# A masked-attention and feed-forward kernel: the causal mask of one half batch, the chunk marks and part of the ELU moved to GpSimd, with new instruction lists

## The chip, the cores and the metric

The kernel runs on one core of a Trainium2 chip. The metric is the device time of one launch in microseconds. The engines are TensorE (PE in the profile, its weight loads PEld), VectorE (DVE), ScalarE (ACT), GpSimd (POOL) and SyncE (SP), which here only issues DMAs.

## The reference

Four batches of eight heads, 768 positions, 64 elements per head. Attention sees, for each query, only the six chunks of 32 keys with the greatest upper bound, under the causal mask; the result goes through a feed-forward layer with an ELU.

```python
k_min, k_max = min, max of k over each chunk of 32      # 24 chunks
ub = sum_d max(q * k_min, q * k_max)                     # [B,H,S,24], later chunks -1e9
top_chunks = argsort(ub)[..., -6:]
scores = q @ k.T / 8
mask = (chunk of key in top_chunks) & (query pos >= key pos)
attn = softmax(where(mask, scores, -1e9))
x = (attn @ v) as [3072, 512]
h = x @ w_in                                             # 512 -> 2048
g = where(h > 0, h, exp(min(h, 0)) - 1)
out = g @ w_out                                          # 2048 -> 512
```

## The kernel before

Heads go in pairs: unit u is a pair of heads, 16 units, four per batch. A unit's queries and each batch's feed-forward layer are cut into two halves of 384 rows.

Per unit there is a preparation. For batch 0 (`first_prep`, per half) keys and queries are loaded in rows and turned by TensorE (L696); ScalarE copies the turned keys (L706) and queries (L728, and L732 with a Relu), VectorE takes minimum and maximum of each chunk (L715), and GpSimd casts queries (L748) and values (L739). For batches 1 to 3 (`pair_prep`) the loads arrive in blocks and VectorE turns them (L615, L633), with the same work behind (L619, L649, L748).

The choice of chunks (`quad_sel`) works for two units at a time: the bounds by TensorE (L782), then VectorE transposes (L798), finds the eight largest (L810), compares (L815) and transposes back (L821), and GpSimd puts the flags of the chunks that are not chosen (L832) into rows 64 to 87 of the query operand. The key operand carries in the same rows the chunk marks, -40000 in row c for keys of chunk c. The score matmul (L874) has these 88 rows, so that a key of a chunk not chosen gets a large negative score. The marks are made once as `econ` (L531) and copied by VectorE into the five buffers of the key operand (L542).

`pair_attend` makes the transposed scores of one half: TensorE writes a piece into PSUM (two buffers S2), ScalarE takes the exponential (L901), TensorE multiplies by the values (L933), VectorE normalises (L946, L949). The diagonal blocks need a triangular mask. In batch 0 (`onpe`) TensorE adds a triangle of -40000 by a second matmul with the identity (L880) into the same bank; in the other batches GpSimd zeroes the triangle behind the exponential by an affine select (L920). The result is turned, by TensorE (L982) and a ScalarE copy (L985), or for some halves through DRAM.

`mlp` makes for each half 16 blocks of 128 features: `up` matmuls (L1011) into one of three PSUM banks H, exponential by ScalarE (L1020), then the ELU in one of three ways. The usual one for batches 0 to 2 takes two VectorE operations that both read PSUM, t = max(e - 1, h) at L1049 and gT = min(max(h, 0), t) at L1054. For the blocks named in `BOTH`, ScalarE makes a Relu in place (L1025) and VectorE one operation (L1028). In batch 3 (`FAST`) two blocks are taken at once in S2: VectorE makes t = min(e, 1) - 1 (L1038), and gT = max(t, h) (L1043). The bank comes free with the last of these. `down` matmuls (L1070) sum 16 blocks into M (MT in batch 3), ScalarE copies (L1079), SP stores.

The order of all this is not left to a scheduler: `QUEUE` lists, for each engine, the numbers of its operations in the order in which it runs them, and each engine works its list strictly from the front. `Plan.order` only places the buffers of the pools by it. The lists of SP (loads and stores) and of GpSimd also hold the DMA issues, among GpSimd's those of the weights (L570, L574), 0.5 MB each.

Of the kernel before, what the change touches and what calls it, by code (L numbers as in the profile page):

```python
# [11 lines left out]
AOT = mybir.AluOpType  # L12
# [5 lines left out]
H = 8  # L18
# [20 lines left out]

BOTH = {0: (1, 5, 9, 13), 1: (0, 1, 2, 3, 4, 5, 8, 9, 10, 11, 12, 13), 2: (1, 5, 9, 13), 3: ()}  # L40
# [7 lines left out]
TRIPE = True  # L48
KCAST = ['ACT', 'ACT']

# [23 lines left out]
    ],  # L74
    "POOL": [
# [10 lines left out]
    ],  # L86
    "ACT": [
# [19 lines left out]
    ],  # L107
# [7 lines left out]
    ],  # L115
# [284 lines left out]
def kernel(  # L400
# [129 lines left out]
    def c_econ():  # L530
        nc.scalar.activation(out=econ[64:96].rearrange("p (c w) -> p c w", w=CHUNK),  # L531
                             in_=ident_f[64:96, 64:64 + NCH].unsqueeze(2).to_broadcast([32, NCH, CHUNK]),
                             func=AF.Copy, scale=MASKNEG)
# [619 lines left out]
```

## Time and profile before

| what | value |
|---|---|
| median of 3 runs | 268.43 us (268.42 to 268.64) |
| profiled execution, first to last instruction | 266.7 us |
| left between the two, outside the span | 1.7 us |
| TensorE busy | 256.0 us, 96% |
| VectorE busy | 211.6 us, 79% |
| ScalarE busy | 195.8 us, 73% |
| GpSimd busy | 118.0 us, 44% |
| HBM over the span | 135 GB/s |

The profile records one execution; no own time is given for it beside its span, so that the span is set against the median of the runs. A group's line shows its source line, engine, operation, output and inputs, shape and count, then its busy time, the mean of one in ns, and the engine's idle time ahead of it with what ended it. A line of the timeline shows the start, the time and the same names. Matmuls are pipelined: one is recorded as busy for longer than the next one has to wait behind it.

### The profile page before, as it was taken

How to read it: one execution, taken by the hardware profiler on the slowest of the kernel's cores; microseconds unless marked ns; L12 is line 12 of the kernel's file. 1: busy time of each engine (PE TensorE's matmuls, PEld its weight loads, DVE VectorE, ACT ScalarE, POOL GpSimd, SP SyncE). 2: the span in 40 equal slices, each digit the busy share in tenths (PEclk: the TensorE clock that was granted, in tenths of full speed). 3: DMA queues.
4: the chain of work that ended last, by engine and by line, in shares of the span. 5: the costliest groups of instructions: out<-in, count | busy, mean ns of one | idle time of the engine just before them, and what ended most of it. 6: DMA issues, size and time to landing. Idle time of an engine off the chain costs nothing.

```text
span 266.7 us, 6618 instructions
## 1 busy us (share of the span) xinstructions
PE 256.0 (96%) x2393; PEld 159.4 (60%) x2420; DVE 211.6 (79%) x544; ACT 195.8 (73%) x363; POOL 118.0 (44%) x208
## 2 busy tenths in 40 slices
PE   4999999999999999999999999999999999999994
PEld 3887766755565556655565555655666555565543
DVE  4897999999999999899997858986779676227640
ACT  4899899955987789997899549787988842433421
POOL 2588774163896898952934157524250000000000
PEclk9999999999999999999999999999999999999999
DMA  6999999999998999999403561040102300210123
GB/s 206 272 238 155 205 194 202 196 147 177 198 153 134 163 204 159 152 167 186 106 7 77 175 172 18 15 125 15 58 11 59 116 2 0 79 42 0 39 81 118
DMA packets 121264, 32.15 MB, mean 121 GB/s; under 512 B 108304, under 2 KB 118288, under 8 KB 121232
## 3 DMA queue, kind: packets, MB, share of 16 engines
q1 hardware_dynamic: 115920, 26.75, 51.3%
q0 software_dynamic: 4224, 4.19, 10.0%
q10 hardware_dynamic: 1088, 0.79, 0.9%
q8 instruction: 19, 0.31, 0.5%
q14 instruction: 13, 0.11, 0.2%
HBM read 28.44 MB, written 7.47 MB: 135 GB/s over the span
## 4 chain that ended last, share of the span: by engine, by line
PE 83%; DVE 5%; ACT 5%; DMA 4%; issue 2%; SPq 0%; DVEq 0%; ACTq 0%
PE psH L1011 20%; PE psM L1070 20%; PE psS L874 11%; PE psS L1011 8%; PE psMT L1070 8%; PE psO L933 7%; PE psS L782 3%; DMA f<-in_v_dram 3%; PE psH L696 2%; PE psMT L696 2%; ACT pt L901 2%; DMA gT<-in_k_dram 1%; ACT lhs L706 1%; PE psT L982 1%; DVE thr L810 1%
## 5 line engine op out<-in xcount | busy, mean ns | idle before, releaser
L901 ACT ACTIVATE pt<-psS 128x768 bf16<-128x768 f32 (+1 forms) x120 | 89.1, 778 | 11.9 <-PE psS L874 7.3
L1011 PE MATMUL psH<-xT,w_in_sb 128*128 128x384 bf16 x384 | 75.0, 326 | 0.3
L1070 PE MATMUL psM<-w_out_sb,gT 128*128 128x512 bf16 x264 | 67.9, 379 | 1.3
L1011 PEld LDWEIGHTS <-w_in_sb 128*128 128x128 bf16 x512 | 47.6, 97 | 34.4 <-issue 1.4
L1070 PEld LDWEIGHTS <-gT 128*128 128x128 bf16 x400 | 37.8, 98 | 34.4 <-DVE gT L1054 0.5
L1020 ACT ACTIVATE f<-psH 128x384 f32<-128x384 f32 x96 | 47.8, 509 | 12.5 <-PE psH L1011 10.1
L920 POOL TENSOR_SCALAR_AFFINE_SELECT pt<-pt 128x512 bf16<-128x512 bf16 (+1 forms) x48 | 24.8, 529 | 69.0 <-ACT pt L901 61.9
L874 PE MATMUL psS<-rhs,lhs 88*128 88x384 bf16 (+4 forms) x304 | 54.2, 283 | 0.8 <-ACT pt L901 0.6
L874 PEld LDWEIGHTS <-lhs 88*128 88x128 bf16 x304 | 27.9, 97 | 15.4 <-ACT pt L901 1.9
L1049 DVE SCALAR_TENSOR_TENSOR t<-f,psH 128x384 bf16<-128x384 f32 x56 | 30.5, 546 | 6.3 <-ACT f L1020 5.8
L748 POOL CAST rhs<-f 64x768 bf16<-64x768 f32 (+1 forms) x40 | 27.9, 702 | 14.1 <-DVE f L633 6.6
L933 PEld LDWEIGHTS <-pt 128*128 128x128 bf16 x672 | 27.5, 98 | 7.5 <-issue 0.9
L1054 DVE SCALAR_TENSOR_TENSOR gT<-psH,t 128x384 bf16<-128x384 f32 x56 | 30.6, 551 | 1.2
L933 PE MATMUL psO<-vext,pt 128*128 128x65 bf16 x672 | 29.6, 194 | 0.2 <-DVE gT L1054 0.2
L748 POOL CAST lhs<-f 64x768 bf16<-64x768 f32 x24 | 19.7, 822 | 18.6 <-PE psS L874 12.3
L832 POOL COPY rhs<-selt 24x576 bf16<-24x576 bf16 (+2 forms) x40 | 22.7, 567 | 8.6 <-DVE selt L821 5.8
L1020 ACT ACTIVATE f<-psS 128x768 f32<-128x768 f32 x16 | 13.0, 811 | 18.0 <-PE psS L1011 17.9
L1028 DVE SCALAR_TENSOR_TENSOR gT<-f,psH 128x384 bf16<-128x384 f32 x40 | 21.4, 542 | 5.3 <-ACT psH L1025 5.3
L1011 PE MATMUL psS<-xT,w_in_sb 128*128 128x384 bf16 x128 | 22.6, 326 | 0.0
L1070 PE MATMUL psMT<-w_out_sb,gT 128*128 128x512 bf16 (+1 forms) x109 | 22.1, 348 | 0.2
L1025 ACT ACTIVATE psH<-psH 128x384 f32<-128x384 f32 x40 | 20.7, 520 | 0.0
L949 DVE TENSOR_TENSOR on<-psO,rc 128x384 bf16<-128x384 f32 x32 | 17.6, 554 | 0.8
(56 smaller groups left out, 270.9 us busy)
## 6 DMA issues: line engine op xcount, KB each, us to landing
out_dram<-osb SPq DMA_DIRECT2D x23, 256.0 KB, 2.5
f<-in_k_dram SPq DMA_DIRECT2D x48, 96.0 KB, 3.9
f<-in_q_dram SPq DMA_DIRECT2D x48, 96.0 KB, 3.8
f<-in_v_dram SPq DMA_DIRECT2D x24, 192.0 KB, 4.0
w_in_sb<-in_moe_w_in_dram POOLq DMA_DIRECT2D x4, 512.0 KB, 7.9
w_out_sb<-in_moe_w_out_dram POOLq DMA_DIRECT2D x4, 512.0 KB, 8.4
gT<-in_k_dram SPq DMA_DIRECT2D x8, 192.0 KB, 4.4
gT<-in_v_dram SPq DMA_DIRECT2D x12, 128.0 KB, 3.9
```

The lines of the kernel that those rows point to most:

```text
L748: nc.gpsimd.tensor_copy(out=o, in_=i)
L832: eng.tensor_copy(out=dst.rearrange("c h (i two x) -> c h i two x", two=2, x=32)[:, :, :, odd, :], in_=tiles[st][r0:r0 + NCH, c0:c0 + n].r ...
L874: nc.tensor.matmul(p_s[:, hd, pc:pc + w], lhsT=tiles[pt_["kb"]][0:64 + NCH, hd, 128 * kb:128 * kb + 128], rhs=tiles[pt_["qb"]][0:64 + NCH, ...
L901: lambda bs=bs, pt=pt, wtot=wtot, lo=lo, at=at: nc.scalar.activation(out=tiles[pt][:, :, lo:lo + wtot], in_=tiles[bs[0]][:, :, at:at + wto ...
L920: nc.gpsimd.affine_select(out=a, in_=a, compare_op=AOT.is_ge, fill=0.0, base=0, pattern=pat, channel_multiplier=-1)
L933: nc.tensor.matmul(po[:, hd, qi, :], lhsT=tiles[pt][:, hd, off:off + 128], rhs=tiles[pt_["vx"]][:, 6 * hd + kb, :], start=(kb == 0), stop= ...
L1011: nc.tensor.matmul(o, lhsT=w_in_sb[:, kk, f0:f0 + 128], rhs=rhs, start=(kk == 0), stop=(kk == NKK - 1))
L1020: lambda e=e, view=view: nc.scalar.activation(out=halves(e)[:, 0:step], in_=view(), func=AF.Exp),
L1028: lambda e=e, view=view, fc=fc, gt=gt: nc.vector.scalar_tensor_tensor(out=tiles[gt][:, fc:fc + step, :], in0=halves(e)[:, 0:step], scalar= ...
L1049: lambda e=e, t=t, view=view: nc.vector.scalar_tensor_tensor(out=tiles[t][:, 0:step], in0=halves(e)[:, 0:step], scalar=1.0, in1=view(), op ...
L1054: lambda t=t, view=view, fc=fc, gt=gt: nc.vector.scalar_tensor_tensor(out=tiles[gt][:, fc:fc + step, :], in0=view(), scalar=0.0, in1=tiles ...
L1070: nc.tensor.matmul(pm, lhsT=tiles[gt][:, fc, 128 * tt:128 * tt + 128], rhs=w_out_sb[:, fc, x0:x1], start=(fc == 0), stop=(fc == NFC - 1))
```

## The change

Four things change. The triangular mask by TensorE stays for the first half of batch 0 alone (`TRIPE`); its second half takes GpSimd's affine select, as the other batches do. The chunk marks are made by GpSimd instead of ScalarE. For 24 blocks of the feed-forward layers of batches 0 to 2 (`POOLED`, four in each half, all of them blocks with two VectorE operations before) GpSimd makes t = min(e, 1) - 1 and VectorE gT = max(t, h). And the lists of all five engines are new; the numbers in them shift, because eight affine selects are added in the plan. The further lines of the diff are a variant of the key copies that is switched off (`KTWO`), tags, and a constant that moves.

```diff
+POOLED = {(0,0):(2,6,10,14),(0,1):(2,6,10,14),(1,0):(6,7,14,15),(1,1):(6,7,14,15),(2,0):(2,6,10,14),(2,1):(2,6,10,14)}
-TRIPE = True
+TRIPE = (0,)
+KTWO = False
 QUEUE = {
...
     def c_econ():
-        nc.scalar.activation(out=econ[64:96].rearrange("p (c w) -> p c w", w=CHUNK),
-                             in_=ident_f[64:96, 64:64 + NCH].unsqueeze(2).to_broadcast([32, NCH, CHUNK]),
-                             func=AF.Copy, scale=MASKNEG)
+        nc.gpsimd.tensor_scalar(out=econ[64:96].rearrange("p (c w) -> p c w", w=CHUNK),
+                                in0=ident_f[64:96, 64:64 + NCH].unsqueeze(2).to_broadcast([32, NCH, CHUNK]),
+                                scalar1=MASKNEG, scalar2=None, op0=AOT.mult)
...
-                onpe = u in SPLIT and TRIPE
+                onpe = u in SPLIT and hf in TRIPE
...
+                if fc in POOLED.get((b, hf), ()):
+                    add("POOL", pool(step * HALF), pr,
+                        lambda e=e, t=t: nc.gpsimd.tensor_scalar(
+                            out=tiles[t][:, 0:step], in0=halves(e)[:, 0:step], scalar1=1.0, scalar2=1.0,
+                            op0=AOT.min, op1=AOT.subtract),
+                        reads=[(e, 0)], writes=[t], alloc=[t], free=[e])
+                    add("DVE", dve(step * HALF), pr,
+                        lambda t=t, view=view, fc=fc, gt=gt: nc.vector.tensor_tensor(
+                            out=tiles[gt][:, fc:fc + step, :], in0=tiles[t][:, 0:step], in1=view(), op=AOT.max),
+                        reads=[t, bh[0]], writes=[(gt, fc + i) for i in range(step)],
+                        alloc=[gt] if fc == 0 else [], free=bh + [t])
+                    continue
```

The new lists, by their beginnings (before, after):

```diff
     "DVE": [
-        0, 6, 11, 9, 12, 8, 10, 22, 23, 38, 7, 39, ...
+        0, 10, 9, 11, 6, 7, 22, 23, 8, 12, 38, 24, ...
     "POOL": [
-        1, 5, 4, 3, 28, 29, 44, 45, 46, 62, 30, 63, 179, 78, 80, 79, 87, 64, 178, 86, 89, 195, 129, 194, 128, 127, 88, 130, 213, 331, ...
+        3, 1, 4, 2, 44, 45, 5, 62, 28, 30, 29, 46, 339, 78, 63, 79, 178, 341, 89, ...
     "SP": [
-        13, 31, 163, 47, 65, 165, 17, 215, 181, 51, 217, 183, 197, 199, 201, 167, 517, ...
+        13, 31, 47, 65, 163, 183, 17, 165, 197, 215, 181, 199, 217, 51, 544, 167, 542, ...
```

Here 2 is `econ`, 6 VectorE's fills of the query operand, 7 the identity's cast, 8 to 12 the copies of the marks, 22 and 23 the first chunk bounds; 331 (before) and 339 (after) the first weight transfer; 17, 51, 167 and 201 loads of values, 517 and 544 the first loads of batch 1, the others of SP loads of keys and queries of batch 0. On TensorE the first `up` of batch 0 stands behind five score pieces of unit 0's second half, one of unit 1's and one value tile before, and behind the five of unit 0 alone after.

More of the change, by code (lines that the diff above doesn't have):

```diff
@@ L47 @@
 PUTS = False
-TRIPE = True
+TURN = ((2, 0), (2, 1), (3, 0),)
+TRIPE = (0,)
 KCAST = ['ACT', 'ACT']
+KTWO = False
 EARLY = (4, 0)
@@ L545 @@
     add("POOL", 0.4, -9.5, c_ident, reads=["fill"], writes=["ident"])
-    add("ACT", 0.7, -9.0, c_econ, reads=["ident"], writes=["econ"])
+    add("POOL", 0.95, -9.0, c_econ, reads=["ident"], writes=["econ"])
     add("POOL", 1.0, -8.9, c_kept, writes=["kept"])
@@ L586, in fetch @@
         add("DMA", 0.0, pr, lambda: None, reads=[w], writes=writes, lat=plan.LANDED)
-    TURN = ((2, 0), (2, 1), (3, 0),)
     PAIR = {}
@@ L687, in first_prep, with kview, turn @@
             fetch(3, 512, 256, pl + 1.55, vload, [(sv, iv), (sv, iv + 1)], alloc=[sv] if u == SPLIT[0] and hf == 0 else [])
-        bk, bq = bank("H"), bank("MT")
-        def turn(bb, i):
+        bk, bq = new("S2") if KTWO else bank("H"), bank("MT")
+        def kview():
+            return tiles[bk[0]][:, 0, 0:HALF] if KTWO else ps(bk, [P, HALF], F32)
+        def turn(view, i, twice=False):
             def f():
-                p_ = ps(bb, [P, HALF], F32)
+                p_ = view()
                 for n in range(3):
@@ L697, in f @@
                                             tiles[sg][:, i, o:o + 64 + 64 * hd], ident_f)
-            return f
-        add("PE", 0.65, pr, turn(bk, i0), reads=[(sg, i0), "ident"], writes=[bk[0]], alloc=bk)
-        for hd in range(2):
+                    if twice:
+                        nc.tensor.transpose(tiles[bk[0]][0:64, 1, 0:HALF].rearrange("p (t j) -> p j t", j=3)[:, n],
+                                            tiles[sg][:, i, 192 + 64 * n:256 + 64 * n], ident_f)
+            return f
+        add("PE", 0.97 if KTWO else 0.65, pr, turn(kview, i0, KTWO), reads=[(sg, i0), "ident"], writes=[bk[0]], alloc=bk)
+        if KTWO:
+            add("ACT", act(S), pr,
+                lambda: nc.scalar.activation(out=tiles[kb][0:64, :, a:b], in_=tiles[bk[0]][0:64, :, 0:HALF], func=AF.Copy),
+                reads=[bk[0]], writes=[(kb, hf, 0), (kb, hf, 1), (bk[0], "turn")], alloc=[] if hf else [kb], tag="ktwo")
+        for hd in () if KTWO else range(2):
             by = KCAST[hf] if hd else "ACT"
@@ L707, in first_prep @@
                         out=o(), in_=ps(bk, None, None)[64 * hd:64 * hd + 64, :], func=AF.Copy),
-                    reads=[bk[0]], writes=w, alloc=al)
+                    reads=[bk[0]], writes=w, alloc=al, tag="kcopy%d" % hd)
             else:
@@ L716, in first_prep @@
                     out=tiles[kx][:, 0:12] if x else tiles[km][:, 0, c],
-                    in_=ps(bk, None, None).rearrange("p (c w) -> p c w", w=CHUNK),
+                    in_=kview().rearrange("p (c w) -> p c w", w=CHUNK),
                     axis=mybir.AxisListType.X, op=op),
@@ L724, in first_prep @@
             reads=[kx, (km, 0, hf)], writes=[(km, 1, hf)], free=[kx], port=True)
-        add("PE", 0.65, pr + 0.05, turn(bq, i0 + 1), reads=[(sg, i0 + 1), "ident"], writes=[bq[0]], alloc=bq,
+        add("PE", 0.65, pr + 0.05, turn(lambda: ps(bq, [P, HALF], F32), i0 + 1), reads=[(sg, i0 + 1), "ident"], writes=[bq[0]], alloc=bq,
             free=[sg] if u == SPLIT[-1] else [])
@@ L728, in first_prep @@
             lambda: nc.scalar.activation(out=tiles[qt][:, a:b], in_=ps(bq, None, None), func=AF.Copy),
-            reads=[bq[0]], writes=[qt], alloc=[qt])
+            reads=[bq[0]], writes=[qt], alloc=[qt], tag="qcopy")
         lo = max(a, SEL0)
@@ L733, in first_prep @@
                                          func=AF.Relu),
-            reads=[bq[0]], writes=[qa], alloc=[qa], free=bq)
+            reads=[bq[0]], writes=[qa], alloc=[qa], free=bq, tag="qrelu")
         for hd in range(2):
```

176 rows, old and new, of the table QUEUE are left out of this document.

## The prediction

> **What bounds the kernel now.** I read the page first, then busy time by stretches, then the order of TensorE's instructions, then the groups by shape. The page's busy shares:
>
> ```profile
> span 266.7 us, 6618 instructions
> PE 256.0 (96%) x2393; PEld 159.4 (60%) x2420; DVE 211.6 (79%) x544; ACT 195.8 (73%) x363; POOL 118.0 (44%) x208
> ```
>
> TensorE is busy 96% of the span; GpSimd has more than half of its time free. The stretches show how that is spread:
>
> ```profile
> 0.00:31.40 31.40, 26.20 (x380) 22.34 (x381) 24.33 (x106) 25.88 (x57) 21.11 (x55) 1.00 1.05 216
> 31.40:60.00 28.60, 28.24 (x308) 18.16 (x309) 26.78 (x62) 24.52 (x47) 14.20 (x23) 1.00 1.25 186
> 60.00:110.00 50.00, 49.39 (x462) 29.41 (x467) 49.44 (x129) 41.96 (x79) 38.68 (x60) 1.00 1.01 166
> ```
>
> The columns are the stretch, its length, then busy time of PE, PEld, DVE, ACT and POOL, the granted clock (1.00 in all), and the DMA. Up to 31.4 us, where the first matmul of the feed-forward part stands, TensorE lacks 5.2 us, 4.0 of them ahead of its first instruction; in the two stretches behind it lacks 0.4 and 0.6. From 60 to 110 VectorE is as full (49.44 of 50) as TensorE (49.39), and GpSimd is at 38.68.
>
> A busy TensorE is not yet one at its peak, because an instruction's end is modelled. What one matmul costs when others queue behind it is the step from start to start:
>
> ```profile
> 30.41 0.22 PE L874 MATMUL psS<-rhs,lhs 88*128 88x128 bf16 x1
> 30.47 0.22 PE L880 MATMUL psS<-trineg,ident_b 128*128 128x128 bf16 x1
> 30.53 0.22 PE L874 MATMUL psS<-rhs,lhs 88*128 88x128 bf16 x1
> 30.59 0.22 PE L880 MATMUL psS<-trineg,ident_b 128*128 128x128 bf16 x1
> 59.75 2.54 PE L1070 MATMUL psM<-w_out_sb,gT 128*128 128x512 bf16 x11
> 62.13 0.81 PE L1011 MATMUL psH<-xT,w_in_sb 128*128 128x384 bf16 x4
> 29.70 0.45 PE L933 MATMUL psO<-vext,pt 128*128 128x65 bf16 x9
> ```
>
> A mask matmul (L880) of 128 columns takes 0.22 us by itself but 0.058 us of the queue (30.41 to 30.59 in three steps: 0.06). In the same way L1070 costs (2.54 - 0.38) / 10 = 0.216, L1011 (0.81 - 0.33) / 3 = 0.161, L933 (0.45 - 0.19) / 8 = 0.032. With these steps I ask how full TensorE really is from 60 to 110:
>
> ```profile
> L1011 PE MATMUL psH<-xT,w_in_sb 128*128 128x384 bf16 x92 | 18.3, 326 | 0.0
> L1070 PE MATMUL psM<-w_out_sb,gT 128*128 128x512 bf16 x69 | 17.8, 379 | 0.4
> L874 PE MATMUL psS<-rhs,lhs 88*128 88x384 bf16 (+2 forms) x78 | 13.7, 288 | 0.1
> L933 PE MATMUL psO<-vext,pt 128*128 128x65 bf16 x138 | 6.0, 194 | 0.2 <-DVE gT L1054 0.2
> L982 PE MATMUL psT<-ident_b,on 128*128 128x128 bf16 x21 | 2.2, 219 | 0.0
> L782 PE MATMUL psS<-f,km 64*32 64x288 f32 x32 | 1.4, 415 | 0.0
> ```
>
> 92 x 0.161 + 69 x 0.216 + 138 x 0.032 + 21 x 0.058 (as the mask's 128 columns) = 35.3. The 78 score matmuls come in widths 384, 256 and 128 as 10 : 4 : 4 and cost by their columns 0.125 on average, 9.8 together. The bound computations (L782) take 1.4 for this operand, and with the other one, which overlaps it, I count 2.3. That is 47.4; for some five L1070 that the trace lacks (a few per cent of the matmul records are missing) I add 1.1. So about 1.5 us of these 50 are waits hidden in busy time; TensorE sets the pace, and VectorE, full as well, is the next that could.
>
> **The change part by part.** First, the mask matmuls of batch 0's second half. Each of its four pairs has three diagonal blocks for two heads, six mask matmuls, 24 in all. Where they lie (columns: PE busy and count, PEld the same):
>
> ```profile
> 26.00:31.40 5.40, 1.06 (x6) 0.58 (x6) 1.00 1.36 201
> 31.40:40.00 8.60, 1.06 (x6) 0.66 (x7) 1.00 1.35 198
> 40.00:50.00 10.00, 1.65 (x9) 0.90 (x10) 1.00 1.36 204
> 50.00:60.00 10.00, 0.47 (x4) 0.20 (x3) 1.00 1.06 158
> ```
>
> Six lie before 31.4, where TensorE has idle time anyway; I take nothing for them (at most 6 x 0.058 = 0.35). The other 18 lie where it has none: 18 x 0.058 = 1.04 us off the path. In their place each pair gets two affine selects on GpSimd, one of 256 and one of 512 elements, between the exponential on ScalarE and the value matmuls. Their price, and that of everything else that moves, stands in the groups by shape:
>
> ```profile
> L920 POOL TENSOR_SCALAR_AFFINE_SELECT pt<-pt 128x512 bf16<-128x512 bf16 x24 | 15.5, 650 | 51.6 <-ACT pt L901 51.0
> L920 POOL TENSOR_SCALAR_AFFINE_SELECT pt<-pt 128x256 bf16<-128x256 bf16 x24 | 9.6, 407 | 17.5 <-ACT pt L901 10.9 <-PE psH L1011 5.2 <-PE psO L933 1.1
> L739 POOL CAST vext<-gT 128x384 bf16<-128x384 f32 x8 | 4.1, 509 | 1.0 <-DMA gT<-in_v_dram 0.9
> L748 POOL CAST lhs<-f 64x768 bf16<-64x768 f32 x24 | 19.7, 822 | 18.6 <-PE psS L874 12.3 <-DVE rc L946 4.6 <-DVE f L615 0.9
> L1049 DVE SCALAR_TENSOR_TENSOR t<-f,psH 128x384 bf16<-128x384 f32 x56 | 30.5, 546 | 6.3 <-ACT f L1020 5.8
> L1054 DVE SCALAR_TENSOR_TENSOR gT<-psH,t 128x384 bf16<-128x384 f32 x56 | 30.6, 551 | 1.2
> ```
>
> Eight selects are 4 x (0.41 + 0.65) = 4.2 us of GpSimd, which has 14.4 free between 31.4 and 60. The select waits on ScalarE; behind it in GpSimd's queue stand the marks and casts of the next pairs, and the value matmuls wait for it. The cover is that score and feed-forward matmuls of other tiles stand between. Without that cover each select would cost TensorE up to its 0.65; I take nothing.
>
> Second, the chunk marks (`econ`) move from ScalarE to GpSimd.
>
> ```profile
> 4.20 0.84 ACT L531 ACTIVATE econ<-ident_f 32x768 bf16<-32x768 f32 x1
> 5.07 1.16 DVE L542 COPY lhs<-econ 32x768 bf16<-32x768 bf16 x4 [2.71 <-ACT econ L531]
> 7.84 0.56 DVE L715 TENSOR_REDUCE km<-psH 128x12 f32<-128x384 f32 x1
> 1.30 1.05 DVE L537 MEMSET rhs<- 32x192 uint32 x5
> 9.35 0.43 DVE L518 CAST ident_b<-ident_f 128x128 bf16<-128x128 f32 x1
> 1.14 0.29 POOL L514 TENSOR_SCALAR_AFFINE_SELECT ident_f<-ident_f 128x128 f32<-128x128 f32 x1 [0.63 <-DVE ident_f L506]
> 1.62 0.36 POOL L528 MEMSET vext<- 128x12 bf16 x5
> 1.83 0.44 POOL L522 MEMSET km<- 128x64 f32 x4
> 2.21 0.58 POOL L524 MEMSET selv<- 128x576 bf16 x1
> ```
>
> Now VectorE waits 2.71 us for the marks, copies them into all five buffers, and only then makes the first chunk bounds at 7.84. ScalarE's 0.84 cost nothing where it stood: its next work waited for TensorE. GpSimd's operation is not in the trace; I bound it by a 64x768 cast (0.82) and the same again (1.64), and take 0.82, the nearest shape. The table load stays, ahead of ScalarE's first activation. In the new lists GpSimd reaches the marks after its fills and the identity, 0.9 + 0.44 + 0.58 + 0.29 + 0.36 = 2.6 us into the span, so they are ready at 3.4. Three buffers' copies (6 x 0.29), the five fills (1.05) and the identity's cast (0.43) then end at 6.6, and the bounds begin 1.2 earlier. But the chain of waits has TensorE's transposes, nearly back to back, from its first row to its row at 11.94:
>
> ```profile
> 3.96 2.79 PE psH L696 x12
> ...
> 11.94 0.49 PE psS L782 x32
> ```
>
> So the gain lies between 0 and 1.2; I take 0.2.
>
> Third, in 24 of the 96 ELU blocks of batches 0 to 2 the step min(e,1)-1 runs on GpSimd, and VectorE's two operations become one. VectorE loses 24 x 0.546 = 13.1 us; the remaining maximum has one PSUM input, like L1054, and keeps about 0.55. GpSimd's new operation is not in the trace: the 128x384 cast gives 0.51 below; the 768-element cast, 0.82, above; I take 0.53, between the selects of 256 and 512. That adds 12.7 us to GpSimd. The chain from exponential to gT keeps its length (0.53 for 0.546), but the block's PSUM bank, one of three, now also waits for its turn in GpSimd's queue, behind casts of 0.82. VectorE's relief is worth between nothing and the 1.5 us of hidden waits from 60 to 110, for the other waits of the stretch are TensorE's; I take 0.4.
>
> The Trainium skill, GPSIMD Engine Reference, section 4.1 (Engine selection), says that GpSimd is about twice as slow as VectorE for two-input operations and near line rate for one input. The new operation has one input; the trace's cast agrees (0.51 for 384 elements against VectorE's 0.55), and by this rule the sum stays. Its section 8 (Key points) says more broadly that VectorE is about twice as fast at elementwise work; the second rival below is what that would make.
>
> Fourth, the lists. Every engine's order is new, but hardly any count is. What I can name: GpSimd issues the first weight transfer after seven of its early casts instead of after seventeen; SP issues all key and query loads of the second half before most value loads; TensorE begins the feed-forward part with five score pieces of pair 0 ahead of it and none of pair 1, where it had one of pair 1 and a value tile. Each of these could move TensorE's early 5.2 us either way. I price the new order at 0, with +-2 us as its uncertainty: somewhat more than the hidden waits of one such stretch (1.5) and less than the early idle time.
>
> The sum: 1.04 + 0.2 + 0.4 = 1.64. The profiled execution has a span of 266.7; the runs have a median of 268.43, and the 1.7 between lie outside the span and are not touched. 268.43 - 1.64 = 266.8.
>
> **The rivals.** (a) The lists are better, too: VectorE's slack lets TensorE close all of the 1.5 us, and the early bounds bring 1.2: 268.43 - 1.04 - 1.5 - 1.2 = 264.7, or about 265.3 if half of the early part comes. For it: VectorE is at 99% from 60 to 110. Against: nothing there says that VectorE ends those waits. Chance 0.17.
>
> (b) Slower: GpSimd is the engine that the blocks wait for. If the new operation takes twice VectorE's 0.546, 1.09 us, GpSimd between 60 and 110 goes from 38.7 to 47 of 50 with the eight blocks that I place there, its queue never empties, and each block holds its bank 0.56 longer. Eight times 0.56 is 4.5 us of TensorE's time; less the 1.64, 271.3. It decides from the point where a block delays TensorE by 1.64 / 24 = 0.07 us on average. For it: three banks only, and in-order casts of 0.82 ahead of a block. Against: the cast's 0.51, and a free GpSimd later on. Chance 0.23.
>
> (c) Slower by the early transfers: the first weights, 0.5 MB, go among the second half's loads. Up to 31.4 the DMA moves 216 GB/s, so those land up to 2.4 us later: 268.43 - 1.64 + 2.4 = 269.2. Against: those loads are issued sooner as well. Chance 0.07.
>
> (d) No change: the matmuls go, and waits on the selects return as much: 268.4. Chance 0.10.
>
> **How the numbers follow.** My forecast has 0.43. Faster by over 0.2% (0.5 us, about what a measurement of this kernel can tell from none) are forecast and (a): 0.60. (d) is 0.10, (b) and (c) 0.30. The range runs from 264.8, which (a) reaches, to 270.8, short of (b)'s full price.
>
> **What would show it.** Right: L880 has 32 matmuls, L1049 32; VectorE falls by about 13 us, GpSimd rises to about 136; the new operation takes near 0.53; TensorE's idle time before its first feed-forward matmul is not longer, and that matmul stands near 31. Wrong: a new operation near 1 us, steps of TensorE lengthened ahead of L1070 or L1011 by waits on VectorE's maximum, GpSimd full from 60 to 110, or early transposes that wait for loads.

## The result and the profile after

The changed kernel takes 281.26 us (280.12 to 282.20, four runs) against 268.43: the ratio is 1.047, 95% interval 1.0434 to 1.0505. Forecast were 266.8 us and a range of 264.8 to 270.8. The page of the changed kernel (`econ` is L540 there, the select L938, GpSimd's new operation L1056, the maximum behind it L1061, `up` L1029):

```profile
span 280.4 us, 6584 instructions
PE 258.3 (92%) x2369; PEld 158.3 (56%) x2396; DVE 199.9 (71%) x520; ACT 197.1 (70%) x362; POOL 159.5 (57%) x241
PEclk9999999999799999999999999999999999999999
PE 46%; POOL 19%; ACT 13%; DVE 10%; DMA 7%; issue 4%; SPq 0%; POOLq 0%; ACTq 0%; DVEq 0%
```

The last line is the chain of work that ended last. The same line of the page before:

```profile
PE 83%; DVE 5%; ACT 5%; DMA 4%; issue 2%; SPq 0%; DVEq 0%; ACTq 0%
```

TensorE was 83% of it; now it is 46%, and GpSimd, which did not appear in it before, is 19%. TensorE is idle for 22.1 us of the span instead of 10.7. The same stretches of time as in the prediction, and the two that follow, show where (the work in a stretch shifts as the kernel gets longer). First two rows of before that the prediction does not show, then the changed kernel:

```profile
110.00:160.00 50.00, 49.65 (x445) 28.85 (x449) 43.65 (x113) 40.13 (x78) 24.92 (x42) 1.00 0.63 131
160.00:210.00 50.00, 49.62 (x461) 30.75 (x467) 40.54 (x99) 42.07 (x76) 18.49 (x31) 1.00 0.20 55
```

```profile
0.00:31.40 31.40, 25.31 (x371) 21.36 (x372) 24.92 (x106) 25.38 (x57) 22.02 (x53) 1.00 1.08 217
31.40:60.00 28.60, 25.92 (x280) 16.25 (x280) 24.00 (x63) 23.06 (x44) 23.24 (x33) 1.00 1.21 181
60.00:110.00 50.00, 46.82 (x437) 27.62 (x443) 42.71 (x92) 39.44 (x71) 39.30 (x56) 0.97 0.78 139
110.00:160.00 50.00, 48.04 (x413) 27.50 (x417) 40.54 (x123) 42.66 (x81) 35.76 (x49) 1.00 0.68 122
160.00:210.00 50.00, 46.62 (x423) 27.78 (x428) 32.70 (x83) 35.32 (x62) 31.79 (x43) 1.00 0.25 65
```

Every stretch from 31.4 to 210 has lost some of TensorE's busy time, 1.6 to 3.0 us. From 160 to 210 GpSimd is only 64% busy, and TensorE still lacks 3.4 us where it lacked 0.4: GpSimd being full is not what it takes. VectorE's busy time has fallen by 11.7 us, near the 13 forecast, and it waits instead. The groups by shape, then the waits (who waited for whom, us in total, times, longest):

```profile
L1056 POOL TENSOR_SCALAR t<-f 128x384 bf16<-128x384 f32 x24 | 35.8, 1492 | 13.2 <-ACT f L1038 12.1 <-POOL rhs L850 0.5
L1061 DVE TENSOR_TENSOR gT<-t,psH 128x384 bf16<-128x384 bf16 x24 | 13.2, 552 | 24.8 <-POOL t L1056 24.8
L1079 DVE SCALAR_TENSOR_TENSOR t<-f,psH 128x384 bf16<-128x384 f32 x32 | 17.3, 545 | 10.6 <-ACT f L1038 10.5
L540 POOL TENSOR_SCALAR econ<-ident_f 32x768 bf16<-32x768 f32 x1 | 2.2, 2159 | 0.1
```

```profile
DVE gT L1061 <- POOL t L1056: 24.8, 19, 3.1
PE psH L1029 <- DVE gT L1061: 7.2, 8, 2.6
```

The waits of TensorE on that maximum from 160 to 210 alone, 3.0 us together:

```profile
PE psH L1029 <- DVE gT L1061: 2.1, 2, 1.6
PE psO L951 <- DVE gT L1061: 0.9, 1, 0.9
```

GpSimd's min and subtract takes 1.49 us, where 0.53 was put in the sum, and the chunk marks 2.16, where it was 0.82. In 19 of 24 blocks VectorE stands and waits for it, 24.8 us together, with its list in order behind. The longest of these waits, in the timeline:

```profile
66.61 0.82 POOL L766 CAST rhs<-f 64x768 bf16<-64x768 f32 x1
67.41 2.94 POOL L1056 TENSOR_SCALAR t<-f 128x384 bf16<-128x384 f32 x2
70.38 0.55 DVE L1061 TENSOR_TENSOR gT<-t,psH 128x384 bf16<-128x384 bf16 x1 [3.10 <-POOL t L1056]
70.98 0.81 PE L1029 MATMUL psH<-xT,w_in_sb 128*128 128x384 bf16 x4 [2.62 <-DVE gT L1061]
72.97 2.67 PE L1029 MATMUL psH<-xT,w_in_sb 128*128 128x384 bf16 x8
```

Two blocks run one behind the other on GpSimd, behind a cast; VectorE can release no bank of H until 70.9; TensorE stops for 2.62 us. The last row shows an after-effect: eight `up` matmuls take (2.67 - 0.33) / 7 = 0.33 us each, about twice their 0.161. The granted clock of this place (columns as before; the last three are clock, DMA share and GB/s):

```profile
68.30:71.00 2.70, 0.08 (x3) 0.01 (x1) 0.62 (x2) 0.47 (x2) 2.64 (x3) 1.00 0.06 9
71.00:75.30 4.30, 4.30 (x16) 2.01 (x16) 3.63 (x6) 2.09 (x4) 4.12 (x7) 0.62 0.01 4
72.00:75.00 3.00, 3.00 (x11) 1.31 (x9) 2.63 (x5) 1.98 (x4) 2.88 (x5) 0.50 0.02 5
```

The idle stretch is followed by one at 0.62 of the clock, 3 us of it at 0.50. The Trainium skill, TensorE: Matmul & The Clock Gate, Part 1 (The HAM clock gate), gives half clock after an idle window of about 3.4 us; here 2.6 us of idle time were enough. The four runs differ in the clock: means of 0.991 and 0.994 go with spans of 280.3 and 280.4 us, 0.997 and 0.999 with 278.6 and 278.3, and since even the last is 11.6 us above the 266.7 of before, the clock is at most a small part of the loss.

### The profile page after: what moved, and what is told of

It is laid out like the page before. It is cut to its first block, busy times and chain, and to the rows that moved or that the text cites. A ratio compares the mean times of both kernels' runs of the same rounds, so it can differ in the third digit from the quotient of the medians.

```text
span 280.4 us, 6584 instructions
## 1 busy us (share of the span) xinstructions
PE 258.3 (92%) x2369; PEld 158.3 (56%) x2396; DVE 199.9 (71%) x520; ACT 197.1 (70%) x362; POOL 159.5 (57%) x241
## 4 chain that ended last, share of the span: by engine, by line
PE 46%; POOL 19%; ACT 13%; DVE 10%; DMA 7%; issue 4%; SPq 0%; POOLq 0%; ACTq 0%; DVEq 0%
PE psH L1029 11%; PE psM L1100 11%; POOL t L1056 8%; PE psS L1029 7%; PE psMT L1100 6%; ACT pt L919 6%; PE psS L892 4%; DMA f<-in_q_dram 4%; POOL pt L938 3%; PE psO L951 3%; POOL rhs L850 3%; POOL lhs L766 2%; ACT f L1038 2%; DVE gT L1061 2%; PE psS L800 2%
## 5 line engine op out<-in xcount | busy, mean ns | idle before, releaser
L919 ACT ACTIVATE pt<-psS 128x768 bf16<-128x768 f32 (+2 forms) x120 | 89.9, 776 | 14.1 <-PE psS L892 11.5
L1029 PE MATMUL psH<-xT,w_in_sb 128*128 128x384 bf16 x384 | 76.6, 329 | 7.5 <-DVE gT L1061 7.2
L1029 PEld LDWEIGHTS <-w_in_sb 128*128 128x128 bf16 x512 | 48.1, 98 | 43.1 <-issue 11.8
L1100 PE MATMUL psM<-w_out_sb,gT 128*128 128x512 bf16 x264 | 69.3, 381 | 1.2
L1056 POOL TENSOR_SCALAR t<-f 128x384 bf16<-128x384 f32 x24 | 35.8, 1492 | 13.2 <-ACT f L1038 12.1
L938 POOL TENSOR_SCALAR_AFFINE_SELECT pt<-pt 128x512 bf16<-128x512 bf16 (+1 forms) x56 | 28.4, 520 | 24.6 <-ACT pt L919 24.1
L951 PEld LDWEIGHTS <-pt 128*128 128x128 bf16 x672 | 31.3, 98 | 13.6 <-issue 1.8
L951 PE MATMUL psO<-vext,pt 128*128 128x65 bf16 x672 | 35.4, 194 | 2.7 <-DVE gT L1061 1.1
L1061 DVE TENSOR_TENSOR gT<-t,psH 128x384 bf16<-128x384 bf16 x24 | 13.2, 552 | 24.8 <-POOL t L1056 24.8
L1079 DVE SCALAR_TENSOR_TENSOR t<-f,psH 128x384 bf16<-128x384 f32 x32 | 17.3, 545 | 10.6 <-ACT f L1038 10.5
L1029 PE MATMUL psS<-xT,w_in_sb 128*128 128x384 bf16 x128 | 22.9, 326 | 0.0
L1100 PE MATMUL psMT<-w_out_sb,gT 128*128 128x512 bf16 (+1 forms) x109 | 22.1, 348 | 0.2
L1068 DVE TENSOR_SCALAR t<-f 128x768 bf16<-128x768 f32 x16 | 8.8, 555 | 17.4 <-ACT f L1038 17.4
```

The costliest lines, as they stand in the source:

```text
L919: lambda bs=bs, pt=pt, wtot=wtot, lo=lo, at=at: nc.scalar.activation(out=tiles[pt][:, :, lo:lo + wtot], in_=tiles[bs[0]][:, :, at:at + wto ...
L938: nc.gpsimd.affine_select(out=a, in_=a, compare_op=AOT.is_ge, fill=0.0, base=0, pattern=pat, channel_multiplier=-1)
L951: nc.tensor.matmul(po[:, hd, qi, :], lhsT=tiles[pt][:, hd, off:off + 128], rhs=tiles[pt_["vx"]][:, 6 * hd + kb, :], start=(kb == 0), stop= ...
L1029: nc.tensor.matmul(o, lhsT=w_in_sb[:, kk, f0:f0 + 128], rhs=rhs, start=(kk == 0), stop=(kk == NKK - 1))
L1056: lambda e=e, t=t: nc.gpsimd.tensor_scalar(out=tiles[t][:, 0:step], in0=halves(e)[:, 0:step], scalar1=1.0, scalar2=1.0, op0=AOT.min, op1=A ...
L1061: lambda t=t, view=view, fc=fc, gt=gt: nc.vector.tensor_tensor(out=tiles[gt][:, fc:fc + step, :], in0=tiles[t][:, 0:step], in1=view(), op= ...
```

## The experiments

My theory after reading this profile: the price of GpSimd's operation alone turned the sign; the rest of the prediction stands. The rivals: the new lists are worse for reasons of their own; the late marks hold up the start; the operation is slow only beside VectorE's work.

### The operations of GpSimd alone

```diff
+for n in (128, 384, 768): GpSimd, three of each, f32 to bf16:
+    tensor_scalar(min 1, subtract 1)      # L30
+    tensor_scalar(min 1)                  # L32
+    tensor_scalar(mult 2)                 # L34
+    tensor_copy                           # L36
+n = 384: bf16 to bf16 (min, subtract)     # L41
+         tensor_scalar(mult 1, add 1)     # L43
+         tensor_tensor(subtract)          # L45
+32 x 768, broadcast (mult)                # L49
```

> This kernel leaves the whole computation out and runs GpSimd operations alone, three of each form, with VectorE idle; its time means nothing, only the durations of its operations do. Theory (the form is slow by itself): min and subtract from f32 to bf16 takes about 1.49 us at 384 elements here too, with nothing beside it, growing with the elements, and the chunk marks' form about 2.16 us. Rival (it is slowed by VectorE's work beside it): about 0.53 us alone. Open in either case: whether one arithmetic operation instead of two (min alone, mult alone) costs as little as the cast, 0.51 us at 384, and whether the types matter.

The groups by shape (mean of one in ns behind the busy time):

```profile
L30 POOL TENSOR_SCALAR o<-a 128x768 bf16<-128x768 f32 x3 | 8.3, 2774 | 0.2
L30 POOL TENSOR_SCALAR o<-a 128x384 bf16<-128x384 f32 x3 | 4.5, 1495 | 0.2
L30 POOL TENSOR_SCALAR o<-a 128x128 bf16<-128x128 f32 x3 | 1.9, 632 | 3.0 <-DMA a<-in_moe_w_out_dram 3.0
L41 POOL TENSOR_SCALAR o<-h 128x384 bf16<-128x384 bf16 x3 | 4.5, 1495 | 0.2
L34 POOL TENSOR_SCALAR o<-a 128x384 bf16<-128x384 f32 x3 | 3.5, 1169 | 0.2
L32 POOL TENSOR_SCALAR o<-a 128x384 bf16<-128x384 f32 x3 | 3.5, 1164 | 0.2
L45 POOL TENSOR_TENSOR o<-a,a 128x384 bf16<-128x384 f32 x3 | 3.0, 992 | 0.2
L43 POOL TENSOR_SCALAR o<-a 128x384 bf16<-128x384 f32 x3 | 1.5, 511 | 0.2
L36 POOL CAST o<-a 128x384 bf16<-128x384 f32 x3 | 1.5, 505 | 0.2
L49 POOL TENSOR_SCALAR o<-a 32x768 bf16<-32x768 f32 x3 | 6.4, 2121 | 0.2
```

The operation is slow by itself: 1.495 us alone, 1.492 in the kernel. Each further element costs (2774 - 632) / 640 = 3.3 ns. Whether the input is f32 or bf16 does not matter (L30, L41). What matters is the pair of operations: one alone, min or mult, costs 1.16, but a multiply followed by an add costs 0.51, as much as a cast. The marks, a multiply alone, cost 2.12 at 768 elements here, too.

### The same lists, with a cast for the operation

```diff
-nc.gpsimd.tensor_scalar(out=t, in0=e, scalar1=1.0, scalar2=1.0, op0=AOT.min, op1=AOT.subtract)
+nc.gpsimd.tensor_copy(out=t, in_=e)
```

> The changed kernel with its lists untouched; only GpSimd's min and subtract of the 24 blocks becomes a cast of the same tile (so the min and the subtraction are left out there). Theory (the price of that operation is what was wrong): the operation falls from 1.49 to about 0.51 us and the kernel from 281.3 to 266 to 268 us, near the prediction. Rival (the new lists are worse for other reasons): it stays above 274 us. Rival (the late chunk marks cost the time): it stays above 277 us.

The group in that kernel:

```profile
L1056 POOL CAST t<-f 128x384 bf16<-128x384 f32 x24 | 12.0, 502 | 16.1 <-ACT f L1038 15.1 <-POOL rhs L850 0.5 <-PE psH L1029 0.2
```

Measured: 265.85 us, ratio 0.9901 (0.9886 to 0.9917). With the price that the prediction had put in, and nothing else changed, the kernel is within 1 us of the 266.8 forecast. The other two rivals are out as the cause of the 12.8 us, since lists, mask and marks were as in the changed kernel.

### The 24 blocks back on VectorE, and the marks back on ScalarE

```diff
-POOLED = {(0,0):(2,6,10,14), ...}
+POOLED = {}     # in VectorE's list each block's first step right ahead of its second
```

> The changed kernel with the 24 blocks' first step back on VectorE, as its usual two operations, each right ahead of the block's second in VectorE's list; all other lists, the mask and the chunk marks as changed. Theory (slow GpSimd operation): 268 to 271 us, since the lists leave VectorE no gap for these 13 us but nothing waits for GpSimd. Rival (lists): 276 us or more.

Measured: 272.07 us, ratio 1.0114 (1.0077 to 1.0152), 1.1 us above the expected range, short of the rival's 276, and 3.6 us above the kernel before: with this work on VectorE the new lists are no gain. Against the kernel with multiply and add below (266.48 us, called the repaired kernel from here on), the 13 us given back to VectorE cost 5.6. My reading is that the lists were made for GpSimd doing this work; no run separates that from the places that I gave the 24 steps in VectorE's list.

```diff
 # on top of it
-nc.gpsimd.tensor_scalar(out=econ ..., scalar1=MASKNEG, op0=AOT.mult)
+nc.scalar.activation(out=econ ..., func=AF.Copy, scale=MASKNEG)
```

> As the kernel with the 24 blocks back on VectorE, and the chunk marks back on ScalarE behind its first four DMA issues. Theory of the late marks: GpSimd made them in 2.16 us, ready at 4.6 us instead of 5.04 on ScalarE, so this changes under 0.5 us either way. Rival (the marks on GpSimd delay the start): 1 to 2 us less than with the marks on GpSimd.

Measured: 272.17 us, 1.0136 (1.0119 to 1.0154): 0.1 us of difference, within what these runs can tell. The slow marks cost nothing that shows at the end.

### A form that GpSimd does fast

Since e - 1 is never below h, min(max(h, 0), e - 1) is the same ELU, and GpSimd's part of it a multiply and an add.

```diff
-nc.gpsimd.tensor_scalar(out=t, in0=e, scalar1=1.0, scalar2=1.0, op0=AOT.min, op1=AOT.subtract)
+nc.gpsimd.tensor_scalar(out=t, in0=e, scalar1=1.0, scalar2=-1.0, op0=AOT.mult, op1=AOT.add)
-nc.vector.tensor_tensor(out=gT, in0=t, in1=h, op=AOT.max)
+nc.vector.scalar_tensor_tensor(out=gT, in0=h, scalar=0.0, in1=t, op0=AOT.max, op1=AOT.min)
```

> The changed kernel, lists untouched, with the same ELU written so that GpSimd has a multiply and an add: t = e * 1 - 1 on GpSimd, gT = min(max(h, 0), t) on VectorE, in VectorE's usual second form. Alone, multiply and add took 0.51 us at 384 elements where min and subtract took 1.50. Theory (the operation's price alone turned the change around): GpSimd's operation 0.51 us, and the kernel within 1 us of the one whose GpSimd step was a cast, 265.9, thus faster than the kernel before by 2 to 3 us. Rival (a real step on GpSimd costs more beside VectorE's work, or the cast's run gained from what it left out): 268 us or more.

The group, the waits for it, and two stretches:

```profile
L1056 POOL TENSOR_SCALAR t<-f 128x384 bf16<-128x384 f32 x24 | 12.2, 510 | 16.4 <-ACT f L1038 15.2 <-POOL rhs L850 0.5 <-PE psH L1029 0.2
```

```profile
DVE gT L1061 <- POOL t L1056: 8.9, 12, 1.8
```

```profile
60.00:110.00 50.00, 49.62 (x490) 30.16 (x495) 47.16 (x114) 43.74 (x80) 39.98 (x64) 1.00 0.97 171
160.00:210.00 50.00, 49.62 (x434) 30.10 (x441) 34.33 (x89) 39.05 (x69) 23.66 (x40) 1.00 0.29 78
```

Measured: 266.48 us, ratio 0.9922 (0.9906 to 0.9937), faster than both kernels. VectorE's waits for GpSimd fall from 24.8 to 8.9 us, and TensorE is full again. From 60 to 110 GpSimd is as busy as in the changed kernel (39.98 and 39.30 us) with more work done; what differs is the length of each operation.

```diff
 # on top of it
-    scalar1=MASKNEG, scalar2=None, op0=AOT.mult)
+    scalar1=MASKNEG, scalar2=0.0, op0=AOT.mult, op1=AOT.add)
```

> As the kernel with multiply and add for the 24 blocks, and the chunk marks written as a multiply and an add of 0 as well. Theory (the fast form is that of the pair, not of the types): the marks fall from 2.16 to about 0.8 us, VectorE's copies start near 3.3 instead of 4.63 us, and the kernel changes by 0 to 0.7 us, since TensorE's transposes go by their own pace until 10 us. Rival (the early start reaches the end): 1.3 us faster.

The marks' group, then VectorE's first rows of the timeline:

```profile
L540 POOL TENSOR_SCALAR econ<-ident_f 32x768 bf16<-32x768 f32 x1 | 0.8, 824 | 0.1
```

```profile
3.30 1.70 DVE L551 COPY lhs<-econ 32x768 bf16<-32x768 bf16 x6 [2.08 <-POOL econ L540]
6.63 0.56 DVE L733 TENSOR_REDUCE km<-psH 128x12 f32<-128x384 f32 x1 [0.36 <-ACT lhs L724]
```

Measured: 266.37 us, 0.9914 (0.9900 to 0.9929). The marks take 0.82, VectorE starts at 3.30 instead of 4.61, and the end moves by 0.1 us, within what these runs can tell.

### A price between

```diff
+GpSimd: t = min(e, 1)        VectorE: gT = max(t - 1, h)      # t rounded to bf16 before the subtraction
```

> The changed kernel, lists untouched, with min(e, 1) alone on GpSimd and (t - 1) max h on VectorE. Alone this single operation took 1.16 us, between 0.51 and 1.50. Theory (each block waits for its operation, and the waits grow faster than the price once GpSimd's queue runs late): above 268.4 and below 281.3; in proportion between 265.9 at 0.50 and 281.3 at 1.49 it would be 276. Rival (a threshold above 1.16): 266 to 268.

The group and the waits for it:

```profile
L1056 POOL TENSOR_SCALAR t<-f 128x384 bf16<-128x384 f32 x24 | 27.9, 1163 | 13.9 <-ACT f L1038 12.8 <-POOL rhs L850 0.5
```

```profile
DVE gT L1061 <- POOL t L1056: 19.1, 18, 2.4
```

Measured: 274.75 us, ratio 1.0226 (1.0213 to 1.0240). With the other two this gives a curve: 266.48 at 0.51 us, 274.75 at 1.16, 281.26 at 1.49. A block that is 0.65 longer costs 8.27 / 24 = 0.34 us, the next 0.33 cost 6.51 / 24 = 0.27: about half of the added length at first, four fifths of it later. By an estimate, drawn straight between the first two, the curve passes 268.5 at some 0.67 us. GpSimd's share of the chain that ended last follows: 1% at 0.51 us, 14% at 1.16, 19% at 1.49.

### One part alone in the old lists

The parts were put into the old lists of GpSimd where their exponentials had ended in the trace of before. First the mask:

```diff
-TRIPE = True
+TRIPE = (0,)      # lists, marks and ELU as before
```

> The kernel before with its own lists, and only the mask of batch 0's second half taken from TensorE; the eight affine selects are put into GpSimd's list where their exponentials ended in the trace of before. Prediction: 18 of the 24 matmuls lie on the path, 1.04 us less: 267.4. Rival (value matmuls wait for the selects as long): 268.4. Rival (GpSimd's list gets late): 269 or more.

A stretch, and two of the waits (L936 are the value matmuls, L923 the selects):

```profile
31.40:60.00 28.60, 27.45 (x289) 17.00 (x290) 26.75 (x59) 24.16 (x46) 18.79 (x31) 1.00 1.21 183
```

```profile
PEld L936 <- POOL pt L923: 0.8, 1, 0.8
PE psO L936 <- POOL pt L923: 0.7, 1, 0.7
```

Measured: 268.49 us, ratio 0.9997 (0.9986 to 1.0009): no change, as the first rival had it. The mask matmuls are gone, TensorE's busy time from 31.4 to 60 falls from 28.24 to 27.45, and the value matmuls wait for a select (0.7 in one wait). In this stretch, what went as work comes back as idle time.

Then the ELU's first step, in the fast and in the slow form:

```diff
-POOLED = {}
+POOLED = {(0,0):(2,6,10,14), ...}    # lists, mask and marks as before
```

> The kernel before with its own lists, mask and chunk marks, and only the first step of the same 24 ELU blocks on GpSimd, in the fast form (multiply and add, 0.51 us); each is put into GpSimd's list where its exponential ended in the trace of before. Prediction's step: VectorE's relief of 13 us is worth 0 to 1.5 us, 0.4 taken: 267 to 268.6. Rival (the relief is what brought the 2 us of the repaired kernel): 266 to 266.7. Rival (the 2 us come from lists that were made for the moved work): no faster than 268.0, or slower, since VectorE's list keeps its old order.

> As the kernel with one part alone in the old lists, but with GpSimd's min and subtract at 1.49 us. Theory (the slow operation holds PSUM banks and TensorE waits, whatever the lists): 278 to 285, some 10 us or more above the same kernel with the fast form. Rival (only the new lists are sensitive): within 4 us of the fast form.

The waits for it, in the fast form and in the slow one:

```profile
DVE gT L1045 <- POOL t L1040: 12.4, 14, 1.8
```

```profile
DVE gT L1045 <- POOL t L1040: 28.0, 20, 2.8
```

Measured: 270.75 us, 1.0091 (1.0074 to 1.0108), and 282.62, 1.0534 (1.0511 to 1.0557). The slow form costs 11.9 us more than the fast one here, and 14.8 in the new lists: the old lists suffer from it, too. And the fast form alone is a loss of 2.2 us, outside of the 267 to 268.6 of the prediction's step: in VectorE's old list the blocks' second step stands where it stood, and VectorE waits there for GpSimd 14 times, 12.4 us together.

### The mask back on TensorE in the new lists

```diff
-TRIPE = (0,)
+TRIPE = (0, 1)    # on top of multiply and add on GpSimd
```

> The repaired kernel (multiply and add on GpSimd for the 24 blocks) in the new lists, with the 24 mask matmuls of the second half back on TensorE and the eight affine selects gone. Prediction's step: 18 matmuls of 0.058 us on the path, so 1.0 us slower than the repaired kernel, 267.5. Rival (as in the old lists, where the mask's move alone gave 0.1 us): within 0.4 us of it.

Measured: 267.35 us, ratio 0.9960 (0.9946 to 0.9974). Against 266.48 the move of the mask is worth 0.9 us in lists that were made for it.

## Why the prediction was wrong

**The step that failed** is the third term: the price of GpSimd's min and subtract. It was not in the trace; I bounded it by casts (0.51 and 0.82) and took 0.53. It is 1.49, outside of both ends. The nearest rows were of another kind: by their two sizes, casts cost 0.8 ns and selects 0.95 ns for each further element, this pair of operations 3.3. The mechanism of rival (b), named with its point of decision, is what happened; I gave it 0.23 and a price of 1.09, and at 1.16 its 271.3 is 274.75. It counted only eight blocks, of the stretch where GpSimd is full; but TensorE lost 3.0 us from 160 to 210, too, where GpSimd was 64% busy, and waited 3.0 us there on VectorE's maximum. The prediction also named only the bank as what waits: it gave no time to VectorE itself, which stands still in its strict list for 24.8 us in all (8.9 with the fast form).

**The rule that I weighed there** was wrong for it as well. The Trainium skill, GPSIMD Engine Reference, section 4.1 (Engine selection), has one-input operations near line rate; the measured 1.16 and 1.49 against a cast's 0.51 speak against it, and only multiply and add (0.51) agrees. Its section 8 (Key points), twice VectorE's time, is nearer and still short: 1.49 / 0.546 is 2.7.

**The rest of the sum held in total, less so term by term.** With the price that the sum had used, the kernel takes 265.85 (a cast) or 266.48 (the repaired ELU), against 266.8. Term by term: the mask, 1.04 forecast, is 0.9 in the new lists (and 0.1 in the old ones, rival (d) on a small scale). The marks were off in price, 2.16 for a bound of 1.64, but at 0.82 the copies start at 3.30 and the bounds at 6.63, as worked out, and the end moves by 0.1, within the noise: the 0.2 that I took for them shows in no run. VectorE's relief, 0.4, has no value of its own: it loses 2.2 in the old lists, and 5.6 are lost when it is undone in the new ones. So the new lists were not worth zero either; relief and lists gained only together, which a sum of separate terms could not show. That the total with the fast form comes within 0.3 us of 266.8 is therefore in part luck: the mask's term is borne out, while relief and lists, 0.4 and 0 in the sum, made some 1 us together.

**What was to be seen.** As forecast: 32 operations at L1079, VectorE down by 11.7 us (13 forecast), the first feed-forward matmul at 30.8, no early transpose that waits for a load but the first. Against: GpSimd at 159.5 instead of 136, the operation at 1.49, and steps of TensorE lengthened by waits on VectorE's maximum, the sign that I had named for a wrong prediction.

**What stays open.** The repaired kernel gains 2 us, 0.9 of them by the mask; how much of the rest is the lists' and how much the moved work's cannot be told, since neither gained without the other. And the 0.6 us between the cast and the repaired ELU are not clear of noise: their intervals, 0.9886 to 0.9917 and 0.9906 to 0.9937, overlap.

## What to carry to other kernels

An operation that the trace does not show was not bounded here by other operations of its engine on as many elements: before work is moved to another engine, time the very form there, and look for an equivalent form, since here min and subtract against multiply and add decided between 281.3 and 266.5 us. Where banks are few and engines take their lists in order, the length of one handed-over operation counts, in this case also on an engine with a third of its time free. And here the moved work gained only with an order made for it: try both together before judging either.

## What was not expected of the hardware

GpSimd's tensor_scalar at 384 elements: 1.16 us with one operation, 1.49 with min and subtract, 0.51 with multiply and add, with nothing beside it; the 992 ns of a subtraction of two tensors lie between. Writing a lone multiply as a multiply and an add of 0 took the marks from 2.14 us to 0.82. And 2.6 us without a matmul were followed by 3 us at a granted clock of 0.50.
